# Reordering the seven products of a blocked matmul stage, with a later unit end and an earlier first store, in a fused spectral + FFN kernel

## The chip, the cores and the metric

One core of one Trainium2 chip runs the whole program. The metric is device time in microseconds from launch to end, as the median of several runs. A profile of one execution gives the span from the first to the last instruction and what each engine did in it. TensorE (PE) multiplies, VectorE (DVE) and ScalarE (ACT) do elementwise work, GpSimd (POOL) mostly issues stores, SyncE (SP) issues loads; DMAs are issued from the queues of SP, ACT and POOL. Each engine takes its instructions strictly in the order of the program.

## The reference, cut to what matters

```python
xn = layernorm(x)                                   # x: 2048 tokens x 1024
s  = irfft2(rfft2(xn) * (w_r + 1j * w_i))           # over tokens and features
h  = silu(xn @ w1)                                  # w1: 1024 x 3584
g  = silu(h @ w2)                                   # w2: 3584 x 1024
return x + s * g
```

## The kernel before

Every float32 operand is split into two float16 parts, high and low, and a product is the sum of three matmuls (high·high, high·low, low·high). The Fourier transforms are matmuls with cosine and sine tables plus butterflies on VectorE. TensorE is fed by one list of instructions that interleaves, stage after stage, the FFN with the spectral part.

**The first FFN product.** The 3584 hidden columns are 14 pairs of blocks, `q` = 0 to 13; the tokens are two halves, `g` = 0 and 1. Pairs 0 to 7 (`NPL` = 8) are computed plainly (`mm1`, line 617). Pairs 8 to 13 are computed by a seven-product scheme for a 2x2 block product: a *unit* is one (q, g), so there are 12 units, with products M1 to M7 each (`product`, line 655). A product is 12 matmuls of 512 columns; there are 84 products. This is the *seven-product stage*.

**What a unit's products need of each other.** A unit has three PSUM tiles: `a` (shown as pa), `e` (pe) and `f` (pc). M1 opens `a`; ScalarE copies it to `f` (line 667); only then may M6 add onto `a`. ScalarE copies that out (line 669) before M7 adds onto `a`; ScalarE copies that out too (line 671) before M4 adds onto `a`. M5 opens `e`, VectorE reads it (line 672), M3 adds onto it and VectorE reads it again (line 679). M2 adds onto `f`. Lines 673, 675, 677 and 680 are the Silu of the four results `h` (pool tag `h32`). PSUM tiles `a` and `e` have two buffers each, so two units can overlap.

**The unit's end.** When M3's result is in, `hidden(q, g)` forms on VectorE three differences `hr` and changes `h` in place (lines 707, 708, 710), and then splits both into high (ScalarE, line 267) and low (VectorE, line 270): the four blocks of `h` into `hoone`, the three of `hr` into `hosum`. Seven stores of 256 KB follow on the POOL queue (line 701), to `hd_one`, `hd_dif`, `hd_sum_0/1` and `hd_sum_d` in DRAM. `hoone`, `hosum` and `hr` have one buffer each.

**What sets the order.** The products stand in a hand-written order: product `name` of unit n is placed at 7·n + its number in `SLOTS`, and all are sorted by that place. After each product, `after(ev)` first runs the *turn*: `settle()` emits the evacuation of the product before, and each step that an earlier step returned, one step per turn. So a function that returns another function delays it by one turn. `tick()` runs deferred stores, and `work()` emits background steps: scaling of weight blocks (lines 267, 270, 435 to 439), maxima of the second weight matrix (`w2max_gen`: 289 on ScalarE, on loads of 256 KB from `in_B_w` into `xn`) and of the spectral weights (line 1162 on VectorE).

**The next stage.** The second FFN product is again seven products (`mm2`, lines 783 to 785, tile pb), the first of which reads only `hd_sum_d`, back from DRAM by `load_h` (line 740; the first seven issued on SP, later ones on ACT). One step of it is 21 matmuls. After five steps TensorE runs the forward transform of tokens 1024 and up (`fa_mat`, line 1016), which needs the cosine table `ca` (512 KB) loaded anew (line 1471, on SP) by `open_fd`, called in `second_half`. ScalarE takes the transform out into `fs` (line 1027). The pool `hid` (with `h32`, `hr`, `hosum`, `hoone`) is closed before that, and the pool `acc`, in which `fs` and the sums `kept` live, takes its place in SBUF.

Of the kernel before, what the change touches and what calls it, by code (L numbers as in the profile page):

```python
# [22 lines left out]
LEAD, PAUSE, EARLY = 2.5, -1, 2  # L23
NPL = 8
KB = 1024
SLOTS = (("M1", 0), ("M6", 2), ("M5", 3), ("M7", 4), ("M2", 5), ("M4", 6), ("M3", 8))
IORDER = (1, 3, 0, 2)
SUMMED, ADDED = (1, 2), (4, 5)
TURNED = (2, 3)
# [112 lines left out]
def spectral_ffn(ctx, tc, x, w_r, w_i, w1, w2, ca, kc, ci, tw, pm, out):  # L142
# [12 lines left out]
    X1 = fp.tile([128, 16 * KB], F32, name="xn")  # L155
    R3 = fp.tile([128, 7 * KB], F32, name="w1")
    hstack = ExitStack()
    H = {"p": hstack.enter_context(tc.tile_pool(name="hid", bufs=1))}
    pf = ctx.enter_context(tc.tile_pool(name="pf", bufs=4, space=PSUM))
    P = {"es": ExitStack()}  # L160
    P["t"] = P["es"].enter_context(tc.tile_pool(name="pt", bufs=2, space=PSUM))
# [25 lines left out]
    def defer(n, fn):  # L187
        deferred.append([n, fn])
# [421 lines left out]
    def mm1(c, f):  # L610
        ps = pf.tile([128, 512], F32, name=f"pa{c}_{f}", tag="ff")
        w, xt = w1t[f], xnT[c]
        terms = [(d, wh, xh) for wh, xh in ((0, 0), (0, 1), (1, 0)) for d in range(8)]
        if c + f:
            terms.sort(key=lambda k: k[0])
        for n, (d, wh, xh) in enumerate(terms):
            nc.tensor.matmul(ps, w[:, wh, d], xt[:, xh, d], start=(n == 0), stop=(n == 23))  # L617
        if c == 3:
            used1.add(f)
            done1.pop(f)()  # L620
        q, g = f // 2, c // 2

        def evac():
            if (q, g) not in h32:
                h32[q, g] = H["p"].tile([128, 4, 512], F32, name=f"h32_{q}_{g}", tag="h32", bufs=2)
            hq = h32[q, g]
            nc.scalar.activation(hq[:, 2 * (c % 2) + f % 2], ps, AF.Silu, scale=ep[:, q:q + 1])  # L627
            if c % 2 and f % 2:
                return hidden(q, g)

        return evac
# [3 lines left out]
    def product(q, g, name):  # L635
# [24 lines left out]
        act, tt = nc.scalar.activation, nc.vector.tensor_tensor  # L660

        def evac():
            if name == "M1":
                h32[q, g] = H["p"].tile([128, 4, 512], F32, name=f"h32_{q}_{g}", tag="h32", bufs=2)
            hq = h32[q, g]
            if name == "M1":
                act(f, a, AF.Copy)  # L667
            elif name == "M6":
                act(hq[:, 0], a, AF.Copy)
            elif name == "M7":  # L670
                act(hq[:, 1], a, AF.Copy)
                tt(hq[:, 1], hq[:, 1], e, op=OP.add)
                return lambda: lambda: (act(hq[:, 1], hq[:, 1], AF.Silu, scale=sc), None)[1]
            elif name == "M4":
                act(hq[:, 3], a, AF.Silu, scale=sc)
            elif name == "M2":
                act(hq[:, 2], f, AF.Silu, scale=sc)
# [6 lines left out]
    def hidden(q, g):  # L684
# [6 lines left out]
        def split(names, src):  # L691
# [5 lines left out]

            def rest():
                low(ov[1], sv, sc, ov[0])
                for k, m in enumerate(names):  # L700
                    defer(1, lambda k=k, m=m: stores[0].dma_start(  # L701
                        hd[m, g][:, :, q].rearrange("f p h s -> f p (h s)"), o[:, k].rearrange("f p h s -> f p (h s)")))

# [9 lines left out]
        summed = ("sum_0", "sum_1", "sum_d"), sums  # L713

        def second():
            a_, b_ = (one, summed) if q >= NPL else (summed, one)
            rest_a = split(*a_)

            def third():
                if q >= NPL:  # L720
                    rest_a()
                    return split(*b_)
                rest_b = split(*b_)
                rest_a()
                return rest_b

            return third

        return second

    stile, queues, fins, sstore = {}, {}, {}, {}
    part, ht = {}, {}
# [297 lines left out]
    def fd_gen(c):  # L1030
# [70 lines left out]
                yield 0  # L1101
        o, sp = {}, {}

        def high_r(j):
            sp[j] = ap.tile([128, 4, 2, 256], F16, name=f"Rs{c}_{j}", tag="Rs", bufs=2)
            nc.scalar.activation(sp[j][:, :, 0], o[j], AF.Copy, scale=2.0**-11)

        def low_r(j):
# [4 lines left out]
                queue.dma_start(vd[j][:, :, c], sp[j])  # L1113
                vcount[j] += 1

            defer(1 if c == 3 or queue is nc.scalar else 2, keep)

        for j in range(4):
            hold_x[0] = hold_x[0] or c == 1
# [346 lines left out]
    def open_fd():  # L1466
        spots = (("E", 0), ("P", 0), ("Q", 2080), ("EE", 4160), ("EO", 6240), ("DS", 8320), ("Rb", 0), ("Rd", 2048), ("Ro", 4160))
        FW[2] = FW[3] = Map({**{k: [(X1, 16 * KB + v)] for k, v in spots}, "V": [(X1, 0)], "Rs": [(X1, 16 * KB + 10400), (R2[0], 60 * KB)],
                             "L0": [(H["scr"], 0)]})
        A["ca"] = view(R2[0], 72 * KB + 256, [128, 2, 8, 128], F16)  # L1470
        nc.sync.dma_start(A["ca"], ca)

    def load_i(c):
        zt = C["p"].tile([128, 4, 2, 2, 8, 64], F16, name=f"zt{c}", tag="zt", bufs=1)
# [186 lines left out]
    with tc.manual_schedule():  # L1661
# [119 lines left out]
        plan = sorted((7 * n + o, n, name) for n in range(len(strassen)) for name, o in SLOTS)  # L1781
        w2j = None
        for n, (_, u, name) in enumerate(plan):
            q, g = strassen[u]
# [40 lines left out]
        steps = [(0, j, k) for k in range(2) for j in range(4)] + [(0, j, k) for j in range(4, 8) for k in range(2)]  # L1825
# [84 lines left out]
```

## Time and profile before

| | us |
|---|---|
| median of 3 runs | 1280.06 (1277.38 to 1281.12) |
| the profiled execution's own time | 1275.51 |
| its span | 1273.7 |
| TensorE busy | 1234.6 (97% of the span) |
| VectorE busy | 992.1 (78%) |
| ScalarE busy | 565.9 (44%) |
| POOL busy | 269.9 (21%) |

The profiled execution is a little shorter than the three timed ones; the span is 1.8 us less than its own time. TensorE matmuls are pipelined, so a product of 12 matmuls shows as 2.75 us but the next starts 2.59 us after it. In the timeline, a row is start, duration, engine, line, operation, and in brackets the idle time before it and what ended it. In the list of waits a row is the waiting instruction, what it waited for, the total, the number of times and the longest.

### The profile page before, as it was taken

The page shows a single profiled execution, that of the slowest core. Times are in us where ns is not written, and L with a number is a line of the kernel's source. Part 1 is how long each engine was busy: PE and PEld are TensorE (multiplying, and loading weights), DVE is VectorE, ACT ScalarE, POOL GpSimd, SP SyncE. Part 2 cuts the span into 40 slices and gives each one's busy share as a digit, 9 for nine tenths or more (in the row PEclk, how much of TensorE's full clock was granted, in tenths as well). Part 3 has the DMA queues.
Part 4 walks back from the last instruction along what each step waited for, and adds up shares of the span by engine and source line. Part 5 has one row for each costly group of instructions (what it writes and reads, how often), then busy time and mean ns, then how long its engine had stood idle before and what let it go on. Part 6 is the DMA issues. An engine that isn't in the chain of part 4 may idle for free. (4 is left out here: it accounts for less than half of the span.)

```text
span 1273.7 us, 18601 instructions
## 1 busy us (share of the span) xinstructions
PE 1234.6 (97%) x6827; PEld 640.0 (50%) x6827; DVE 992.1 (78%) x1646; ACT 565.9 (44%) x844; POOL 269.9 (21%) x428
## 2 busy tenths in 40 slices
PE   8999999999999998999999999999899989999998
PEld 5544444444444443444445455555455456566654
DVE  6677998889987876877487959996799338976875
ACT  4855465664447776766323223332234213412221
POOL 1221243523233231332200000202122400110111
PEclk9999999999999999999999999999899999999999
DMA  7469698867578878856946888979999998977687
GB/s 237 130 161 227 161 307 223 235 174 214 125 191 240 258 232 265 266 170 204 317 146 187 256 252 212 323 232 289 201 284 285 344 353 296 312 281 281 226 271 264
DMA packets 184187, 306.68 MB, mean 241 GB/s; under 512 B 32032, under 2 KB 92448, under 8 KB 182944
## 3 DMA queue, kind: packets, MB, share of 16 engines
q1 hardware_dynamic: 138176, 163.85, 42.9%
q0 software_dynamic: 30128, 92.82, 25.5%
q10 hardware_dynamic: 15792, 48.83, 10.9%
q8 instruction: 53, 0.87, 0.3%
q14 instruction: 38, 0.31, 0.1%
HBM read 204.25 MB, written 111.67 MB: 248 GB/s over the span
## 5 line engine op out<-in xcount | busy, mean ns | idle before, releaser
L617 PE MATMUL pa<-xn,w 128*128 128x512 f16 x1536 | 335.2, 381 | 5.8 <-DVE w L270 2.5
L783 PE MATMUL pb<-r,w 128*128 128x512 f16 (+1 forms) x798 | 299.8, 376 | 1.0 <-DMA w<-hd_one 1.0
L784 PE MATMUL pb<-r,w 128*128 128x512 f16 (+1 forms) x798 | 299.8, 376 | 0.0
L785 PE MATMUL pb<-r,w 128*128 128x512 f16 (+1 forms) x798 | 299.7, 376 | 0.0
L617 PEld LDWEIGHTS <-w 128*128 128x128 f16 x1536 | 150.1, 98 | 186.9 <-issue 3.9
L655 PEld LDWEIGHTS <-w 128*128 128x128 f16 x1008 | 98.5, 98 | 131.5 <-issue 12.5
L785 PEld LDWEIGHTS <-w 128*128 128x128 f16 x798 | 78.0, 98 | 91.2
L783 PEld LDWEIGHTS <-w 128*128 128x128 f16 x798 | 78.1, 98 | 86.9 <-DMA w<-hd_one 1.5
L784 PEld LDWEIGHTS <-w 128*128 128x128 f16 x798 | 78.0, 98 | 85.3
L655 PE MATMUL pa<-r,w 128*128 128x512 f16 x432 | 99.1, 379 | 11.0 <-ACT pc L667 7.5
L267 ACT ACTIVATE r<-r,sc 128x512 f16<-128x512 f32 x88 | 61.1, 715 | 101.4 <-DMA r<-in_B_w_dram 70.0
L270 DVE SCALAR_TENSOR_TENSOR r<-r,sc 128x512 f16<-128x512 f32 x88 | 65.1, 747 | 35.4 <-ACT r L267 35.2
L701 POOL DMA_DIRECT2D hd_one<-hoone x52 | 45.6, 876 | 199.3 <-DVE hoone L270 111.4
L701 POOL DMA_DIRECT2D hd_sum<-hosum x52 | 42.7, 932 | 158.1 <-DVE hosum L270 101.7
L270 DVE SCALAR_TENSOR_TENSOR hoone<-h,hs,hoone 128x2048 f16<-128x2048 f32 x28 | 65.7, 2345 | 8.0 <-ACT hoone L267 7.8
L267 ACT ACTIVATE hoone<-h,hs 128x2048 f16<-128x2048 f32 x28 | 55.9, 1995 | 21.7 <-DMA hd_one<-hoone 12.2
L267 ACT ACTIVATE hosum<-hr,hs 128x1536 f16<-128x1536 f32 x28 | 44.0, 1570 | 28.6 <-DVE hr L708 23.9
L627 ACT ACTIVATE h<-pa,ep 128x512 f32<-128x512 f32 x64 | 42.9, 676 | 29.5 <-PE pa L617 28.0
L270 DVE SCALAR_TENSOR_TENSOR hosum<-hr,hs,hosum 128x1536 f16<-128x1536 f32 x28 | 50.7, 1811 | 1.2 <-ACT hosum L267 1.2
L1228 PE MATMUL fx<-xn 128*128 128x256 f16 x192 | 45.2, 280 | 5.2 <-DMA xn<-vd 5.2
L1495 PE MATMUL iu<-xn 128*128 128x256 f16 x384 | 46.2, 279 | 3.2 <-DVE xn L1505 2.7
L707 DVE TENSOR_TENSOR hr<-h 128x1024 f32<-128x1024 f32 x28 | 34.2, 1220 | 17.5 <-ACT h L627 14.2
(292 smaller groups left out, 2041.4 us busy)
## 6 DMA issues: line engine op xcount, KB each, us to landing
w<-hd_dif ACTq DMA_DIRECT2D x32, 448.0 KB, 6.3
r<-in_B_w_dram SPq DMA_DIRECT2D x56, 256.0 KB, 8.6
w<-hd_sum ACTq DMA_DIRECT2D x32, 448.0 KB, 6.8
w<-hd_one ACTq DMA_DIRECT2D x32, 448.0 KB, 6.8
hd_sum<-hosum POOLq DMA_DIRECT2D x52, 256.0 KB, 5.2
hd_one<-hoone POOLq DMA_DIRECT2D x52, 256.0 KB, 4.6
hd_dif<-hoone POOLq DMA_DIRECT2D x52, 256.0 KB, 4.2
xn<-in_B_w_dram SPq DMA_DIRECT2D x40, 256.0 KB, 5.1
```

The lines of the kernel that those rows point to most:

```text
L267: nc.scalar.activation(hi, raw, AF.Copy, scale=scale)
L270: nc.vector.scalar_tensor_tensor(lo, raw, scale, hi, op0=OP.mult, op1=OP.subtract)
L617: nc.tensor.matmul(ps, w[:, wh, d], xt[:, xh, d], start=(n == 0), stop=(n == 23))
L627: nc.scalar.activation(hq[:, 2 * (c % 2) + f % 2], ps, AF.Silu, scale=ep[:, q:q + 1])
L655: nc.tensor.matmul(ps, lhs(d, wh), rhs(d, xh), start=(name in ("M1", "M5") and d + n == 0), stop=(d + n == 5), skip_group_check=True)
L701: defer(1, lambda k=k, m=m: stores[0].dma_start(hd[m, g][:, :, q].rearrange("f p h s -> f p (h s)"), o[:, k].rearrange("f p h s -> f p (h ...
L707: tt(sums[:, 0:2], hq[:, 0::2], hq[:, 1::2], op=OP.subtract)
L783: nc.tensor.matmul(ps, hh[:, 0], w[:, 0], start=first, stop=False)
L784: nc.tensor.matmul(ps, hh[:, 0], w[:, 1], start=False, stop=False)
L785: nc.tensor.matmul(ps, hh[:, 1], w[:, 0], start=False, stop=last)
L1228: nc.tensor.matmul(o, k[:, c, kh, 1], v[:, c, vh], start=(n == 0), stop=False)
L1495: nc.tensor.matmul(ps[:, q], lhs, rhs, start=(n == 0 and r == 0), stop=(n == 2 and r == 1))
```

## The change

`SLOTS` gets other numbers. Taken in turn, a unit n in mid-stage went M1(n), M3(n-1), M6(n), M5(n), M7(n), M2(n), M4(n); now it goes M1(n), M4(n-1), M3(n-1), M6(n), M5(n), M7(n), M2(n). `FINAL`, used for the last unit, holds the same numbers. `h` is allocated at M6 and not at M1. `hidden` returns its splitting step one turn later for the pairs from 8 on; for the last unit it splits `hosum` ahead of `hoone`; within `hosum` the store to `hd_sum_d` comes first, for all units. The cosine table is asked for in `second_half` once `ready2` is 11 and not 13, with one pause fewer afterwards. The pool `hid` is split: `h32` stays in it, the rest goes to a pool `ho` behind it; and `fs` gets a pool of its own, `scr`, ahead of `acc`. `kept_r` makes sure that the store of a spectral tile is issued before its buffer is written again.

```diff
-SLOTS = (("M1", 0), ("M6", 2), ("M5", 3), ("M7", 4), ("M2", 5), ("M4", 6), ("M3", 8))
+SLOTS = (("M1", 0), ("M6", 3), ("M5", 4), ("M7", 5), ("M2", 6), ("M4", 8), ("M3", 9))
+FINAL = (("M1", 0), ("M6", 3), ("M5", 4), ("M7", 5), ("M2", 6), ("M4", 8), ("M3", 9))
...
-    H = {"p": hstack.enter_context(tc.tile_pool(name="hid", bufs=1))}
+    H = {"h": hstack.enter_context(tc.tile_pool(name="hid", bufs=1)), "p": hstack.enter_context(tc.tile_pool(name="ho", bufs=1))}
...
-            if name == "M1":
-                h32[q, g] = H["p"].tile([128, 4, 512], F32, name=f"h32_{q}_{g}", tag="h32", bufs=2)
-            hq = h32[q, g]
+            if name == "M6":
+                h32[q, g] = H["h"].tile([128, 4, 512], F32, name=f"h32_{q}_{g}", tag="h32", bufs=2)
+            hq = h32.get((q, g))
...
-                for k, m in enumerate(names):
+                for k, m in sorted(enumerate(names), key=lambda t: t[1] != "sum_d"):
                     defer(1, lambda k=k, m=m: stores[0].dma_start(
...
-            a_, b_ = (one, summed) if q >= NPL else (summed, one)
+            a_, b_ = (one, summed) if q >= NPL and (q, g) != (NP - 1, 1) else (summed, one)
             rest_a = split(*a_)
             def third():
-                if q >= NPL:
+                if a_ is one:
                     rest_a()
                     return split(*b_)
...
-        return second
+        return (lambda: second) if q >= NPL else second
...
+        kept_r = {}
+
         def high_r(j):
+            if j - 2 in kept_r:
+                kept_r.pop(j - 2)()
...
-        A["ca"] = view(R2[0], 72 * KB + 256, [128, 2, 8, 128], F16)
-        nc.sync.dma_start(A["ca"], ca)
...
     def second_half():
-        while not p2[0] or ready2[0] < 13:
+        while not p2[0] or ready2[0] < 11:
+            yield PAUSE
+        A["ca"] = view(R2[0], 72 * KB + 256, [128, 2, 8, 128], F16)
+        nc.sync.dma_start(A["ca"], ca)
+        yield PAUSE
+        while ready2[0] < 13:
             yield PAUSE
         open_fd()
-        for _ in range(3):
+        for _ in range(2):
             yield PAUSE
...
-        for _ in range(6):
+        for _ in range(7):
             settle()
             tick()
         hstack.close()
         reopen("pu")
         H["es"] = ExitStack()
+        scr_pool = H["es"].enter_context(tc.tile_pool(name="scr", bufs=1))
+        H["scr"] = scr_pool.tile([128, 2080], F32, name="fs")
         acc_pool = H["es"].enter_context(tc.tile_pool(name="acc", bufs=1))
-        H["scr"] = acc_pool.tile([128, 2080], F32, name="fs")
```

How the instructions then stand, at three places. A name is tile_q_g_serial, or tile_buffer_serial; line numbers after the change are up to a few higher for the same statement (671 is 672, 289 is 290).

ScalarE before, from the copy of M7 of unit (11, 1) to the copy of M6 of unit (12, 0):

```order
L671 ACTIVATE h_11_1_4457<-pa_1_4420 128x512
L267 ACTIVATE hoone_11_0_4538<-h_11_0_4302,hs 128x16x128
L677 ACTIVATE h_11_1_4457<-pc_1_4422,ep 128x512
L267 ACTIVATE hosum_11_0_4556<-hr_0_4515,hs 128x12x128
L289 ACTIVATE both,ma<-r_2498 128x512 x2
L675 ACTIVATE h_11_1_4457<-pa_1_4420,ep 128x512
L673 ACTIVATE h_11_1_4457<-h_11_1_4457,ep 128x512
L289 ACTIVATE both,ma<-r_2498 128x512 x2
L667 ACTIVATE pc_0_4570<-pa_0_4568 128x512
L289 ACTIVATE both,w2m<-xn 128x512 x2
L669 ACTIVATE h_12_0_4606<-pa_0_4568 128x512
```

Here `hosum`, two Silus and two pairs of 289 stand between the split of `hoone` and M1's copy (667). ScalarE at the same place after:

```order
L672 ACTIVATE h_11_1_4498<-pa_1_4397 128x512
L678 ACTIVATE h_11_1_4498<-pc_1_4399,ep 128x512
L268 ACTIVATE hoone_11_0_4559<-h_11_0_4342,hs 128x16x128
L290 ACTIVATE both,ma<-r_2501 128x512 x2
L668 ACTIVATE pc_0_4545<-pa_0_4543 128x512
L674 ACTIVATE h_11_1_4498<-h_11_1_4498,ep 128x512
L268 ACTIVATE hosum_11_0_4582<-hr_0_4518,hs 128x12x128
L290 ACTIVATE both,ma<-r_2501 128x512 x2
L676 ACTIVATE h_11_1_4498<-pa_1_4397,ep 128x512
L290 ACTIVATE both,w2m<-xn 128x512 x2
L670 ACTIVATE h_12_0_4646<-pa_0_4543 128x512
```

M1's copy (now 668) has moved ahead of the Silu of M7, of `hosum`, of a pair of 290 and of the Silu of M4; these now stand between it and the copy of M6 (670).

POOL before, the last unit's stores, with the last one of the unit ahead of it:

```order
L701 DMA hd_sum_d_82<-hosum_13_0_5120 512x1x256
L701 DMA hd_one_1_93<-hoone_13_1_5151 512x1x256
L701 DMA hd_dif_1_85<-hoone_13_1_5151 512x1x256
L701 DMA hd_dif_1_87<-hoone_13_1_5151 512x1x256
L701 DMA hd_one_1_91<-hoone_13_1_5151 512x1x256
L701 DMA hd_sum_1_95<-hosum_13_1_5154 512x1x256
L701 DMA hd_sum_1_89<-hosum_13_1_5154 512x1x256
L701 DMA hd_sum_d_83<-hosum_13_1_5154 512x1x256
```

Here `hd_sum_d` is the last of all. POOL at the same place after:

```order
L702 DMA hd_sum_0_91<-hosum_13_0_5138 512x1x256
L702 DMA hd_sum_d_86<-hosum_13_1_5154 512x1x256
L702 DMA hd_sum_1_98<-hosum_13_1_5154 512x1x256
L702 DMA hd_sum_1_92<-hosum_13_1_5154 512x1x256
L702 DMA hd_one_1_96<-hoone_13_1_5156 512x1x256
L702 DMA hd_dif_1_88<-hoone_13_1_5156 512x1x256
L702 DMA hd_dif_1_90<-hoone_13_1_5156 512x1x256
L702 DMA hd_one_1_94<-hoone_13_1_5156 512x1x256
```

The store of `hd_sum_d` has moved from seventh to first of the last unit's seven. SP before, around the cosine table:

```order
L740 DMA w_67<-hd_sum_d_82 128x1792 x4
L555 DMA r_2498<-wt_4_154 128x512
L555 DMA r_2498<-wt_5_155 128x512
L1471 DMA r_2498<-in_ca_dram 128x2048
L555 DMA r_2498<-wt_6_156 128x512
```

and after:

```order
L741 DMA w_67<-hd_sum_d_85 128x1792 x4
L556 DMA r_2501<-wt_4_157 128x512
L556 DMA r_2501<-wt_5_158 128x512
L1655 DMA r_2501<-in_ca_dram 128x2048
L556 DMA r_2501<-wt_6_159 128x512
```

The load of the table stands behind the same four loads of `hd_sum_d` and the same two of `wt` as before; on SP nothing has moved here. On TensorE nothing has moved outside the seven-product stage.

More of the change, by code (lines that the diff above doesn't have):

```diff
@@ L662, in evac @@
         def evac():
-            if name == "M1":
-                h32[q, g] = H["p"].tile([128, 4, 512], F32, name=f"h32_{q}_{g}", tag="h32", bufs=2)
-            hq = h32[q, g]
+            if name == "M6":
+                h32[q, g] = H["h"].tile([128, 4, 512], F32, name=f"h32_{q}_{g}", tag="h32", bufs=2)
+            hq = h32.get((q, g))
             if name == "M1":
@@ L1114, in keep @@
                 vcount[j] += 1
-            defer(1 if c == 3 or queue is nc.scalar else 2, keep)
+            kept_r[j] = keep
+            defer(1 if c == 3 or queue is nc.scalar else 2, lambda: kept_r.pop(j, int)())
         for j in range(4):
@@ L1780, in spectral_ffn @@
         strassen = [(q, g) for q in range(NPL, NP) for g in range(2)]
-        plan = sorted((7 * n + o, n, name) for n in range(len(strassen)) for name, o in SLOTS)
+        plan = sorted((7 * n + o, n, name) for n in range(len(strassen)) for name, o in (SLOTS if n + 1 < len(strassen) else FINAL))
         w2j = None
```

## The prediction

> **What bounds the kernel now.** I read the page's first part to see which engine is the bound.
>
> ```profile
> span 1273.7 us, 18601 instructions
> ...
> PE 1234.6 (97%) x6827; PEld 640.0 (50%) x6827; DVE 992.1 (78%) x1646; ACT 565.9 (44%) x844; POOL 269.9 (21%) x428
> ```
>
> TensorE is idle for 1273.7 − 1234.6 = 39.1 us, and the change takes away no matmul. So everything that it can win lies in those 39 us, and it wins it only where TensorE stops waiting. The second view is TensorE's list of waits, which says for what it stops.
>
> ```profile
> PE pa L655 <- ACT pc L667: 7.5, 5, 2.7
> PE fx L1228 <- DMA xn<-vd: 5.2, 2, 5.0
> PE iu L1495 <- DVE xn L1505: 2.7, 1, 2.7
> ...
> PE fa L1016 <- DMA r<-in_ca_dram: 2.3, 1, 2.3
> PE pa L655 <- ACT h L669: 2.0, 2, 1.2
> ...
> PE pa L655 <- ACT h L671: 1.5, 1, 1.5
> ```
>
> Four of these six rows are in reach of the diff. Line 655 is the seven-product stage: five stops of M6 for M1's copy (667), two of M7 for M6's copy (669), one of M4 for M7's copy (671), 11.0 us in all. Line 1016 is the transform that waits for the cosine table. The third view is TensorE's timeline over the stage: its ends, and the stops of which I speak below.
>
> ```profile
> 374.29 2.75 PE L655 MATMUL pa<-xn,w 128*128 128x512 f16 x12
> ...
> 377.77 2.76 PE L655 MATMUL pa<-r,w 128*128 128x512 f16 x12 [0.73 <-ACT pc L667]
> ...
> 403.38 2.75 PE L655 MATMUL pa<-r,w 128*128 128x512 f16 x12 [1.25 <-ACT h L669]
> ...
> 485.38 2.75 PE L655 MATMUL pa<-r,w 128*128 128x512 f16 x12 [1.54 <-ACT h L671]
> ...
> 534.34 2.75 PE L655 MATMUL pa<-r,w 128*128 128x512 f16 x12 [2.71 <-ACT pc L667]
> ...
> 601.68 2.75 PE L655 MATMUL pe<-xn,w 128*128 128x512 f16 x12
> 604.27 0.38 PE L783 MATMUL pb<-r,w 128*128 128x512 f16 x1
> ```
>
> The stage takes 604.27 − 374.29 = 229.98 us. A product that nothing disturbs takes 604.27 − 601.68 = 2.59, and 84 of them 217.56. So 12.4 us are lost here, of which the waits name 11.0; the other 1.4 over eight stops are 0.18 each, in which the pipeline of matmuls fills again.
>
> Why the copy is late is seen on ScalarE ahead of the longest stop, at 534.34.
>
> ```profile
> 525.85 2.00 ACT L267 ACTIVATE hoone<-h,hs 128x2048 f16<-128x2048 f32 x1 [3.54 <-DVE h L710]
> 527.76 0.67 ACT L677 ACTIVATE h<-pc,ep 128x512 f32<-128x512 f32 x1
> 528.33 1.56 ACT L267 ACTIVATE hosum<-hr,hs 128x1536 f16<-128x1536 f32 x1
> 529.79 0.62 ACT L289 ACTIVATE both<-r 128x512 f16<-128x512 f32 x1
> ...
> 531.16 0.67 ACT L675 ACTIVATE h<-pa,ep 128x512 f32<-128x512 f32 x1
> 531.73 0.71 ACT L673 ACTIVATE h<-h,ep 128x512 f32<-128x512 f32 x1
> 532.35 0.62 ACT L289 ACTIVATE both<-r 128x512 f16<-128x512 f32 x1
> ...
> 533.72 0.58 ACT L667 ACTIVATE pc<-pa 128x512 f32<-128x512 f32 x1
> ```
>
> ScalarE first stands 3.54 us for `hidden`'s last difference (710), and then works without a gap until the copy. TensorE asked for that copy at 534.34 − 2.71 = 531.63.
>
> **The change, part by part.**
>
> *The order of the seven products.* M6 keeps its place in the row, and M1 moves one product ahead of where it was: M4 now stands behind M1 and not ahead of it. So M1's copy has two products, 5.2 us, and had one. M7's copy likewise has two (M2 and M1 of the next unit) before M4, and had one. M6's copy still has one, M5, before M7. I walk the heaviest boundary, above, through the new order of ScalarE, with starts differenced from its rows. The split of `hoone` starts no sooner than 525.85, since the products that `hidden` follows have not moved, and takes 527.76 − 525.85 = 1.91; a pair of 289 takes 531.16 − 529.79 = 1.37; then the copy, 0.58, is done at 527.76 + 1.37 + 0.58 = 529.7. M6's turn is at 531.63: 1.9 us to spare, and 0.5 where a second pair stands there. So the 667 stops go, apart from the 0.73 at 377.77, which is the first unit, with no unit ahead of it to move behind: 7.5 − 0.7 = 6.8. The 671 stop at 485.38 goes too, 1.5: the added product is 2.59 and the stop 1.54. With five stops go five refills, 5 x 0.18 = 0.9. Together **−9.2**.
>
> What is late next is the copy of M6, because the work that stood ahead of 667 now stands behind it. Behind 529.7 come a Silu (673) 0.62, the split of `hosum` 1.46, a pair 1.37, a Silu (675) 0.57, a pair 1.37 and the copy 0.58: 535.7. M6 itself, 2.75 long, ends at 534.4, and M7's turn is at 531.63 + 2 x 2.59 = 536.8. That leaves 1.1 us, and −0.3 where another pair falls in between. The stop at 403.38 stays: 289 there waited for a load, as its row says, and 669 is behind it in both orders.
>
> ```profile
> 402.13 0.63 ACT L289 ACTIVATE both<-xn 128x512 f16<-128x512 f32 x1 [1.25 <-DMA xn<-in_B_w_dram]
> ```
>
> For the new M7 waits the trace has no row. Below: none, if each boundary is like the one walked. Above: two like 403.38 and one extra pair, 2 x 1.25 + 1.37 = 3.9. I take **+0.7**, two stops of 0.3 each with some refill, as only boundaries with a pair more than the walked one are short.
>
> *The unit's end one turn later.* The splits then no longer stand in ScalarE's row at the moment when 710 is still running, so the 3.54 us of standing go into useful work; the walk has that in it. The stores follow a product, 2.59, later, and `hoone` and `hosum`, with one buffer each, are taken again 18 us later (seven products), so they hide. `h` allocated at M6 moves no instruction: zero.
>
> *The last unit's end and the cosine table.* Here is the end of the stage, on SP, POOL, ScalarE and TensorE, with the time from the table's issue to its landing.
>
> ```profile
> 604.25 10.02 SPq L740 DMA_DIRECT2D w<-hd_sum_d  x4
> ...
> 615.61 0.43 SPq L1471 DMA_DIRECT2D r<-in_ca_dram  x1
> ```
>
> ```profile
> 615.31 0.71 POOL L701 DMA_DIRECT2D hd_one<-hoone  x1 [6.81 <-DVE hoone L270]
> ...
> 619.08 1.36 POOL L701 DMA_DIRECT2D hd_sum_d<-hosum  x1
> ```
>
> ```profile
> 613.01 1.58 ACT L267 ACTIVATE hosum<-hr,hs 128x1536 f16<-128x1536 f32 x1 [0.38 <-DMA hd_sum_d<-hosum]
> ...
> 629.87 0.72 ACT L267 ACTIVATE r<-r,sc 128x512 f16<-128x512 f32 x1 [12.84 <-DMA hd_sum_d<-hosum]
> ```
>
> ```profile
> 629.44 0.22 PE L1016 MATMUL fa<-r,xn 128*128 128x128 f16 x1 [2.35 <-DMA r<-in_ca_dram]
> ```
>
> ```profile
> DMA to landing us min/median/max: 13.7/13.7/13.7
> ```
>
> ```profile
> 620.00:625.00 5.00, 5.00 (x25) 2.26 (x24) 0.00 (x0) 0.00 (x0) 0.44 (x1) 1.00 1.02 380
> ```
>
> SP cannot go past the loads of `hd_sum_d` until that block is stored, 604.25 to about 613, and the table's load stands behind them. The order shows it at the same place after: asking when `ready2` is 11 moves nothing on SP, so the edit by itself is worth zero. What changes is what lies beside it. The table is issued at 615.61 and lands 13.7 later, at 629.3, because the DMA engines are full (share 1.02 in the last row) with the last unit's seven stores, issued from 615.31, among others. After, `hd_sum_d` of the unit ahead is stored as first of its three, and not as last, so SP is free at least as soon. The last unit's split of `hosum`, now first, can still not start before its buffer's stores land, near 613.0; 1.58 on ScalarE and about as much on VectorE put the first store 1 to 2 us later than 615.31, and the four `hoone` stores some 3 us behind the first. So the table's load has the queues to itself for its first microseconds. Bounds for its landing time: 13.7 again, and the median of loads of the same 512 KB elsewhere:
>
> ```profile
> w<-in_B_w_dram SPq DMA_DIRECT2D x17, 512.0 KB, 6.1
> ```
>
> TensorE comes at 629.44 − 2.35 = 627.1, 11.5 us after the issue. The middle of 6.1 and 13.7 is 9.9, which is in time. So the stop goes with its refill: **−2.5**; at 13.7 it stays.
>
> A rule of the Trainium skill bears on this, "DMA: Bandwidth & Descriptors", section "Queues, rings and completion order": each DMA engine takes turns, packet by packet, between the queue rows that have work for it. By it the table on SP's row shared with POOL's row almost from its issue before, and has less to share with afterwards, so the stop would go (−11.0 in all); by the one row there is, 13.7, it would stay (−8.5). The share of 1.02 agrees that the engines were full; no row tells whose packets went first.
>
> The store of `hd_sum_d` as the last unit's first ends ScalarE's 12.84 us of standing early. That costs TensorE nothing now, since ScalarE's next work for it (1027) follows the stopped 1016, and it gains nothing by itself. Splitting the pools lets `fs` be cleared without waiting for those stores: VectorE only, hidden behind the five steps of `mm2` that TensorE does meanwhile, zero; and if that cover went, it is no more than the 2.35 already counted. The seventh turn puts an `mm2` step ahead of the pool's closing only in program order, not on TensorE: zero. `kept_r` issues a store at the latest when its buffer is rewritten; behind the stage it moves nothing on SP's or POOL's queue: zero.
>
> Sum: −9.2 − 2.5 + 0.7 = **−11.0 us**. The profiled execution took 1275.51, so it would take 1264.5; it lies 4.55 below the median of 1280.06, and from the median the forecast is **1269**.
>
> **The rivals.**
>
> *The table stays late.* It lands 13.7 us after its issue again, or the loads that share SP's queue hold it. Then the −2.5 falls away: −8.5, 1271.6. For it: the DMA engines stay full, since all the bytes still have to move. Against it: the stores start later.
>
> *Given back later.* All that follows starts 11 us sooner, but loads do not get faster. The next long stop is for a load:
>
> ```profile
> 917.37 0.37 PE L1228 MATMUL fx<-xn 128*128 128x256 f16 x1 [5.03 <-DMA xn<-vd]
> ```
>
> ```profile
> 918.00:920.00 2.00, 2.00 (x16) 1.73 (x15) 1.35 (x2) 0.86 (x2) 0.17 (x1) 0.50 1.08 320
> 950.00:1000.00 50.00, 50.00 (x266) 25.07 (x265) 39.75 (x66) 15.15 (x28) 21.98 (x45) 1.00 0.99 305
> ```
>
> The engines are full at 950 to 1000 (share 0.99), and after a stop of 5.03 the granted clock is 0.50. If that stretch is set by its bytes, the stop grows by what is gained ahead of it: all 11 us come back, and one more spell at half clock, some 2 us, may come with it: 1278 to 1282, middle 1280. For it: the stop is there and the engines are full. Against it: TensorE is busy 97%, so the loads mostly keep up, and what feeds this stop is issued when earlier work on the same engines is done, which moves forward with it.
>
> *Slower: M7 waits in every unit.* The moved work stands ahead of 669 at all 11 boundaries, and each pair of 289 may itself wait for its load.
>
> ```profile
> ACT h L671 <- PE pa L655: 21.5, 9, 4.0
> ACT h L669 <- PE pa L655: 16.3, 9, 4.0
> ACT both L289 <- DMA xn<-in_B_w_dram: 10.3, 6, 4.8
> ```
>
> The walk left 1.1 us. For the result to be slower than before by 0.3% (3.84 us, about what a measurement of this kernel can tell from no change) the new waits must come to 11.0 + 0.7 + 3.8 = 15.5, 1.4 per boundary, so ScalarE must be 2.5 us later than in the walk at each: 1284 or more. For it: six waits of 289 for a load, up to 4.8 us. Against it: at nine of the 12 units ScalarE stood at 669 waiting for TensorE, 16.3 / 9 = 1.8 us each, so it is ahead there at most boundaries.
>
> **How the numbers follow.** The forecast, 1269, gets 0.66; the table still late, 1271.6, 0.13; given back, 1280, 0.14; slower, 1284 or more, 0.04; 0.03 is for a gain larger than I can see. The forecast's own range: M7 waits from 0 to 3.9 in place of 0.7 give 1268.3 to 1272; the scatter of the three runs, 1277.4 to 1281.1, adds 2 or 3 us on each side. From 1263 to 1277 holds the first two cases and the smaller part of "given back". Faster by over 0.3% is below 1276.2: the first two, the last, and a small part of the third: 0.84. Within 0.3%: 0.11. Slower: 0.05.
>
> **What would show it.** In the trace after, the 667 row of TensorE's waits should hold one stop of 0.7; the 671 row should be gone; 669 should hold 2 to 5 stops and under 4 us; from the stage's first product to the first `mm2` matmul should be 221 to 222 us. The load of the table should be issued about 11 us after that point and land within 11.5 us, with no stop at 1016. The `vd` stop at 1228 should be about 5 us still. The prediction is wrong if the 669 row rises above 4 us or the stops in 850 to 1050 grow by what the stage gained.

## The result, and the profile after

The changed kernel takes 1269.15 us (median of 9 runs, 1266.86 to 1271.73); the kernel before, over nine runs, 1278.55. The ratio is 0.9931, with a 95% interval of 0.9916 to 0.9947: 8.8 us faster, between 6.8 and 10.7. Measured a second time, the same kernel gave 1269.98 and a ratio of 0.9935 (0.9913 to 0.9957).

TensorE is again read first, by the page's first part:

```profile
span 1265.8 us, 18607 instructions
...
PE 1232.4 (97%) x6827; PEld 639.3 (51%) x6827; DVE 991.6 (78%) x1646; ACT 567.0 (45%) x844; POOL 272.5 (22%) x428
```

The span fell by 1273.7 − 1265.8 = 7.9 us. TensorE's list of waits from the stage's start to past the transform has only two rows left (line numbers are one higher than before):

```profile
PE pa L656 <- ACT pc L668: 2.6, 2, 1.9
PE pa L656 <- ACT h L670: 2.2, 4, 0.8
```

The row for M7's copy (671 before) and the row for the cosine table are gone. In TensorE's timeline, the stage's ends, the stops that matter and the transform:

```profile
375.96 2.75 PE L656 MATMUL pa<-xn,w 128*128 128x512 f16 x12
379.44 2.76 PE L656 MATMUL pa<-r,w 128*128 128x512 f16 x12 [0.73 <-ACT pc L668]
...
492.65 2.75 PE L656 MATMUL pa<-r,w 128*128 128x512 f16 x12 [1.87 <-ACT pc L668]
...
599.27 0.38 PE L784 MATMUL pb<-r,w 128*128 128x512 f16 x1
...
621.93 0.22 PE L1017 MATMUL fa<-r,xn 128*128 128x128 f16 x1
```

The 7.9 us divide into four stretches. The stage takes 599.27 − 375.96 = 223.31, and took 229.98: −6.7. From its end to the transform it is 621.93 − 599.27 = 22.66, and was 629.44 − 604.27 = 25.17: −2.5. Ahead of the stage it is 375.96 − 374.29 = +1.7, where the edit moves nothing on TensorE, and behind the transform 643.87 against 644.26: −0.4. The last two are within the scatter of profiles: over the fourteen of this study the stage begins between 373.56 and 376.45, and a second profile of the changed kernel began its stage at 375.40, took 222.31 for it, 22.66 to the transform and 645.83 behind it.

The table's load (SP), the last unit's first store (POOL) and the load's time to landing:

```profile
610.44 0.38 SPq L1655 DMA_DIRECT2D r<-in_ca_dram  x1
```

```profile
613.34 0.71 POOL L702 DMA_DIRECT2D hd_sum_d<-hosum  x1 [8.65 <-DVE hosum L271]
```

```profile
DMA to landing us min/median/max: 10.2/10.2/10.2
```

Counted from the stage's end, the load is issued at 11.2 us (before 11.3), the stores start at 14.1 (before 11.0), and the table lands at 21.4, ahead of TensorE at 22.7.

### The profile page after: what moved, and what is told of

Read it like the earlier page. It is cut to its first block, busy times and chain, and to the rows that moved or that the text cites. A ratio compares the mean times of both kernels' runs of the same rounds, so it can differ in the third digit from the quotient of the medians.

```text
span 1265.8 us, 18607 instructions
## 1 busy us (share of the span) xinstructions
PE 1232.4 (97%) x6827; PEld 639.3 (51%) x6827; DVE 991.6 (78%) x1646; ACT 567.0 (45%) x844; POOL 272.5 (22%) x428
## 5 line engine op out<-in xcount | busy, mean ns | idle before, releaser
L268 ACT ACTIVATE hoone<-h,hs 128x2048 f16<-128x2048 f32 x28 | 55.8, 1994 | 14.1 <-DMA hd_one<-hoone 8.0
L702 POOL DMA_DIRECT2D hd_sum_d<-hosum x26 | 23.6, 907 | 165.3 <-DVE hosum L271 107.9
L708 DVE TENSOR_TENSOR hr<-h 128x1024 f32<-128x1024 f32 x28 | 34.2, 1220 | 14.3 <-ACT h L628 13.1
```

The lines of the kernel that those rows point to most:

```text
L268: nc.scalar.activation(hi, raw, AF.Copy, scale=scale)
L702: defer(1, lambda k=k, m=m: stores[0].dma_start(hd[m, g][:, :, q].rearrange("f p h s -> f p (h s)"), o[:, k].rearrange("f p h s -> f p (h ...
```

## Experiments

The first question was which part of the edit is worth what. Each of its main parts was done alone on the kernel before, or undone alone in the changed kernel; the table's earlier request and `kept_r` were not run by themselves. The stage runs from its first product to the first `mm2` matmul in each profile, in us, and "to transform" from there to the first matmul of line 1016. These two columns come from one execution each; the ratio comes from several runs.

| kernel | stage | to transform | ratio of times to before |
|---|---|---|---|
| before | 229.98 | 25.17 | 1 |
| changed | 223.31 | 22.66 | 0.9931 (0.9916 to 0.9947) |
| changed, second profile | 222.31 | 22.66 | 0.9935 (0.9913 to 0.9957) |
| order alone | 229.43 | 24.21 | 0.9974 (0.9954 to 0.9995) |
| changed, old order | 230.37 | 22.66 | 0.9977 (0.9956 to 0.9998) |
| changed, old turn of the unit's end | 229.14 | 22.67 | 0.9966 (0.9949 to 0.9984) |
| last unit's sums first, alone | 230.52 | 22.66 | 1.0009 (0.9987 to 1.0031) |
| changed, last unit's sums as before | 224.99 | 25.76 | 0.9976 (0.9961 to 0.9991) |
| changed, old pools | 224.30 | 22.66 | 0.9961 (0.9938 to 0.9985) |
| two products in all hand-overs | 232.72 | 27.79 | 1.0039 (1.0018 to 1.0061) |
| changed, without maxima in the stage | 222.15 | 22.66 | 0.9887 (0.9857 to 0.9918) |
| changed, maxima one step later | 224.12 | 22.66 | 0.9906 (0.9882 to 0.9930) |

**The order alone.**

```diff
-SLOTS = (("M1", 0), ("M6", 2), ("M5", 3), ("M7", 4), ("M2", 5), ("M4", 6), ("M3", 8))
+SLOTS = (("M1", 0), ("M6", 3), ("M5", 4), ("M7", 5), ("M2", 6), ("M4", 8), ("M3", 9))
```

> The kernel before with the new order of the seven products alone (and h allocated at M6). Theory: the stage loses most of its stops for 667 and 671 by the order alone, so from its first product to the first mm2 matmul it takes 222 to 225 us (before 229.98, after the change 223.31), the stop for the cosine table stays at 2 to 3 us, and the time is 5 to 7 us below before. Rival: the order alone does little, because without the later unit end the split of hoone still stands on ScalarE waiting for line 710 ahead of M1's copy; then the stage stays at 227 to 230 us and the time within 3 us of before.

The rival held for the stage: it is 229.43, 0.6 us shorter than before. The time is 2.9 us below before by the medians, at the edge of the rival's 3. The order takes 3.1 us off the stops for M1's copy (7.5 before), but those for M6's copy grow by 2.7 (2.0 before; TensorE's waits):

```profile
PE pa L655 <- ACT h L669: 4.7, 3, 1.9
PE pa L655 <- ACT pc L667: 4.4, 5, 1.9
```

ScalarE at the boundary from unit (11, 1) to (12, 0):

```profile
527.90 2.00 ACT L267 ACTIVATE hoone<-h,hs 128x2048 f16<-128x2048 f32 x1 [3.16 <-DVE h L710]
529.81 0.67 ACT L677 ACTIVATE h<-pc,ep 128x512 f32<-128x512 f32 x1
530.38 1.56 ACT L267 ACTIVATE hosum<-hr,hs 128x1536 f16<-128x1536 f32 x1
...
533.22 0.58 ACT L667 ACTIVATE pc<-pa 128x512 f32<-128x512 f32 x1
```

ScalarE stands 3.16 us for line 710, and both splits are still ahead of M1's copy. The extra product covers some of it, but not this. In the whole stage ScalarE stands 13.7 us for line 710, and stood 7.6 before.

**The later unit end alone**, that is, the changed kernel with the old `SLOTS` in place (`FINAL` likewise).

```diff
-SLOTS = (("M1", 0), ("M6", 3), ("M5", 4), ("M7", 5), ("M2", 6), ("M4", 8), ("M3", 9))
+SLOTS = (("M1", 0), ("M6", 2), ("M5", 3), ("M7", 4), ("M2", 5), ("M4", 6), ("M3", 8))
```

> The changed kernel with the old order of the seven products; later unit end, last unit, pools as changed. Theory (order and later end are worth something only together): the split of hosum and two pairs of line 290 still stand ahead of M1's copy with one product to cover them, so the stage stays at 226 to 230 us, the transform's stop stays away, and the time is 3 to 6 us above the changed kernel's. Rival (the later end alone does it, since ScalarE no longer stands waiting for line 711): the stage is at 222 to 225 us.

The theory held. The stops for M1's copy are as large as in the kernel before (7.5):

```profile
PE pa L656 <- ACT pc L668: 7.4, 5, 2.6
PE pa L656 <- ACT h L670: 2.7, 2, 1.8
```

ScalarE's waits in the stage no longer hold a row for `hidden`'s last difference (711 here), but the split of `hosum` (here 492.36) still precedes the copy (495.19), which has one product to cover it:

```profile
492.36 1.56 ACT L268 ACTIVATE hosum<-hr,hs 128x1536 f16<-128x1536 f32 x1
...
495.19 0.58 ACT L668 ACTIVATE pc<-pa 128x512 f32<-128x512 f32 x1
```

**The later unit end undone.**

```diff
-        return (lambda: second) if q >= NPL else second
+        return second
```

> The changed kernel with the unit's end at its old turn (the split steps not one turn later). Theory: the split of hoone stands on ScalarE waiting for line 711 ahead of M1's copy again, at some of the boundaries, so 668 stops of 1 to 3 us in total come back and the stage takes 224 to 226 us; the table's stop stays away; the time is 0 to 3 us above the changed kernel's. Rival: the added product covers that as well, and the stage stays at 223.3 or below, with the stops left being those of line 290 for its loads.

The theory had the direction and too small a size: the stage is back at 229.14, 5.8 us above the changed kernel's. ScalarE stands 15.5 us for line 711 (4.0 in the changed kernel), and stops of all three kinds are there again (TensorE's waits):

```profile
PE pa L656 <- ACT pc L668: 4.9, 5, 1.9
PE pa L656 <- ACT h L670: 4.0, 3, 1.6
PE pa L656 <- ACT h L672: 1.2, 1, 1.2
```

So in the stage the order and the later end gain 0.6 and −0.4 us each by itself, less than the 1.0 by which two profiles of the changed kernel differ, and 6.7 together. The order alone leaves ScalarE standing for line 710; the later end alone leaves `hosum` ahead of a copy that one product covers. Of these kernels, only the changed one has `hosum` behind M1's copy at the boundaries near 492 and 527.

**The last unit's sums first, alone.**

```diff
-                for k, m in enumerate(names):
+                for k, m in sorted(enumerate(names), key=lambda t: t[1] != "sum_d"):
...
-            a_, b_ = (one, summed) if q >= NPL else (summed, one)
+            a_, b_ = (one, summed) if q >= NPL and (q, g) != (NP - 1, 1) else (summed, one)
```

> The kernel before with the last unit's sums split and stored first and hd_sum_d stored first of the sums; order of the products, unit's end and pools as before. Theory (the table lands in time because the last unit's stores start later): the sums must wait for their buffer, so the stores start 1 to 3 us later than 11.0 us after the stage's end, the table lands in 9 to 12 us and its stop of 2.35 us falls to 0 to 1.2; the stage stays at 230, the time is 1 to 2.5 us below before. Rival (the table's earlier request or the split pools did it): the stop stays at 2 to 2.5 us and the time is that of before.

The theory held for the table: it lands 10.0 us after its issue, and that stop is gone. It failed for the time, which is that of before. TensorE's next matmul for the transform stops instead, because VectorE clears `fs`, and ScalarE then copies into it, only when the last store of `hd_one` has landed (VectorE's and TensorE's timelines):

```profile
631.31 0.10 DVE L1026 MEMSET fs<- 128x8 f32 x2 [9.51 <-DMA hd_one<-hoone]
```

```profile
632.48 0.22 PE L1016 MATMUL fa<-r,xn 128*128 128x128 f16 x1 [2.83 <-ACT fs L1028]
```

**The last unit's sums as before, in the changed kernel.**

```diff
-                for k, m in sorted(enumerate(names), key=lambda t: t[1] != "sum_d"):
+                for k, m in enumerate(names):
...
-            a_, b_ = (one, summed) if q >= NPL and (q, g) != (NP - 1, 1) else (summed, one)
+            a_, b_ = (one, summed) if q >= NPL else (summed, one)
```

> The changed kernel with the last unit's four blocks of h split and stored first and hd_sum_d last, as before; the later unit end, the table's request and the pools stay changed. Theory (the stores' start decides): the stores start sooner than 14.1 us after the stage's end, at 11 to 12.5, the table's landing goes back to 12 to 14 us and a stop of 1 to 2.5 us at the transform returns; the time is 1 to 2.5 us above the changed kernel's. Rival (the later unit end alone delays the stores enough, or the split pools did it): no stop, same time as the changed kernel.

The theory held, with a larger stop than it gave. From the stage's end (599.40) the stores start at 11.9 us and the table is asked for at 12.5; it takes 13.1 to land, and TensorE stops for it:

```profile
611.29 0.71 POOL L702 DMA_DIRECT2D hd_one<-hoone  x1 [6.48 <-DVE hoone L271]
```

```profile
DMA to landing us min/median/max: 13.1/13.1/13.1
```

```profile
PE fa L1017 <- DMA r<-in_ca_dram: 2.9, 1, 2.9
```

The later unit end is in this kernel, so it isn't what holds the stores back; the order of the sums is. The time rose by 4 to 6 us, against the 1 to 2.5 expected: the stretch up to the transform (25.76 against 22.66) explains 3.1, and the stage of this one profile is 1.7 to 2.7 longer than in the two of the changed kernel, for which no cause was looked for.

**The pools as before, in the changed kernel.**

```diff
-    H = {"h": ...tile_pool(name="hid", bufs=1)), "p": ...tile_pool(name="ho", bufs=1))}
+    H = {"p": ...tile_pool(name="hid", bufs=1))}
+    H["h"] = H["p"]
...
-        H["scr"] = scr_pool.tile([128, 2080], F32, name="fs")
+        H["scr"] = acc_pool.tile([128, 2080], F32, name="fs")
```

> The changed kernel with the pools as before: one pool for h, hr and the splits, and fs in the pool acc. Theory (from the run with the last unit's sums first alone, where TensorE stopped 2.83 us at the transform for fs, whose clearing on VectorE waited for the last store of hd_one): the table lands in time, and a stop of 2 to 3.5 us at the transform for the copy into fs takes its place; the time is 2 to 4 us above the changed kernel's. Rival (the prediction's zero for this part): no stop there, the time is that of the changed kernel.

The theory held. `fs` shares its pool with tiles that take the place of those still being stored, and waits for them; TensorE stops for it at the transform (VectorE's timeline; TensorE's waits):

```profile
627.48 0.10 DVE L1028 MEMSET fs<- 128x8 f32 x2 [9.22 <-DMA hd_one<-hoone]
```

```profile
PE fa L1018 <- ACT fs L1030: 3.5, 1, 3.5
```

In the changed kernel the clearing waits for no store. The stop is 3.5 us; the time, against the changed kernel's second measurement on the same chip, is 0.9961 to 0.9935, some 3 us, with intervals that overlap.

**Two products in all three hand-overs.** A try at a better order.

```diff
-SLOTS = (("M1", 0), ("M6", 3), ("M5", 4), ("M7", 5), ("M2", 6), ("M4", 8), ("M3", 9))
+SLOTS = (("M1", 0), ("M6", 3), ("M5", 5), ("M7", 6), ("M2", 8), ("M4", 9), ("M3", 11))
```

> The changed kernel with an order of the products in which all three hand-overs (M1 to M6, M6 to M7, M7 to M4) have two products between: M1(n), M2(n-1), M4(n-1), M6(n), M3(n-1), M5(n), M7(n). Theory (what is left of the stage's stops is one product too little of cover at M7, and loads that line 290 waits for): the 670 stops go but for the first unit, M1's copy stands right behind M7's on ScalarE so the 668 stop near 492 goes, the stage takes 218.5 to 221.5 us and the time is 2 to 5 us below the changed kernel's. Rival (the later M3 pushes the unit's end and its stores into the next unit's hand-overs, or makes TensorE wait for h or for pe): the stage stays at 222 to 226 us and the time is that of the changed kernel or above.

The rival held, by more than it gave: the stage, 232.72, is above its 226, and the kernel is slower than before. Of the longer stretch to the transform, 4.5 us are a sixth step of `mm2` that TensorE does there, in place of five. The stops moved to M7 (TensorE's waits, then ScalarE ahead of the longest, at 462.99):

```profile
PE pa L656 <- ACT h L670: 11.0, 5, 4.0
```

```profile
446.05 0.58 ACT L668 ACTIVATE pc<-pa 128x512 f32<-128x512 f32 x1 [0.88 <-PE pa L656]
449.69 0.63 ACT L290 ACTIVATE both<-r 128x512 f16<-128x512 f32 x1 [3.06 <-DMA r<-in_B_w_dram]
...
453.13 0.63 ACT L290 ACTIVATE both<-xn 128x512 f16<-128x512 f32 x1 [1.97 <-DMA xn<-in_B_w_dram]
...
462.36 0.58 ACT L670 ACTIVATE h<-pa 128x512 f32<-128x512 f32 x1
```

Between the two copies ScalarE now has four pairs of 290, both splits and three Silus, and stood 5.0 us for loads: together more than the two products cover.

**The changed kernel again**, with no edit.

> The changed kernel itself once more, for the scatter of its stops. Theory: the stops at the same three or four places of the stage (near 385, 404 and 492 us) come again, within 1 us in total, since the loads that line 290 waits for come in the same order; stage 222.5 to 225 us, no stop at the transform. Rival: the stop near 492 is chance and goes; stage 221 to 222 us.

The theory held: stops at 384.74, 403.88 and 491.52, the last of 1.90. The small ones near 478 and 534 did not come again, and the stage, 222.31, is 0.2 us under the range.

**Without the maxima.** Two kernels, the changed one and the one with two products in all hand-overs, put constants in place of the results of line 290 by writes on VectorE where the maxima stood.

```diff
-            magnitude(t_.rearrange("p a b -> p (a b)"), w2m[:, 2 * n:2 * n + 2])
+            nc.vector.memset(w2m[:, 2 * n:2 * n + 2], 1.0)
...
-                magnitude(r[i].rearrange("p a b -> p (a b)"), ma[:, 2 * i:2 * i + 2])
+                nc.vector.memset(ma[:, 2 * i:2 * i + 2], 1.0)
```

> The changed kernel without the absolute maxima on ScalarE (the pairs of line 290) of the second weight matrix and of the first one's last blocks in the stage; constants stand in their place, the loads stay. Theory (what is left of the stage's stops is ScalarE standing in those pairs for their loads): the 668 stop near 492 and the 670 stops go, apart from the first unit's 0.7 at 668 and at most 0.5 at 670; the stage takes 218 to 219.5 us. Rival (the splits and Silus behind M1's copy are themselves too long for M7): 670 stops stay, and the stage takes 220.5 to 222 us.

> The order with two products in all three hand-overs, also without those maxima (constants in their place, loads kept). Theory (that order lost because the pairs of line 290 come to stand between M1's and M6's copies and wait there for their loads): its 670 stops of 4.0, 3.0 and 2.1 us go, the stage takes 218 to 220 us and not 232.7. Rival (the splits of hoone and hosum and the Silus alone make M6's copy late): 670 stops of 1 us and more stay, the stage is above 222.

Neither tells what it was meant to. The stages are 228.07 and 234.02, single times 1271.78 and 1284.54, and ScalarE came to wait for those very writes, which stand in VectorE's row behind its own waits (ScalarE's waits in the first):

```profile
ACT h L670 <- DVE w2m L477: 5.1, 1, 5.1
```

So the constants were set once at the program's start, and nothing was written in the stage:

```diff
     w2m = small("w2m", 2 * NFT)
+    nc.vector.memset(w2m, 1.0)
...
-            magnitude(t_.rearrange("p a b -> p (a b)"), w2m[:, 2 * n:2 * n + 2])
+            pass
...
-                magnitude(r[i].rearrange("p a b -> p (a b)"), ma[:, 2 * i:2 * i + 2])
+                pass
```

> The changed kernel without the maxima of line 290 in the stage, as in after_no_maxima, but with nothing written in their place there (the constants are set once, at the program's start), since in that run ScalarE and TensorE came to wait for the constants' writes on VectorE. The loads stay. Theory (what is left of the stage's stops is ScalarE standing in those pairs for their loads): the 668 stop near 492 goes, the 670 stops go but for the first unit's, the stage takes 218 to 220 us and the time is 2 to 5 us below the changed kernel's. Rival (the splits and Silus alone, or buffers of h that come free late, make the copies late): stops of more than 1 us stay behind the first unit, the stage takes 221 us or more.

It came out between the two. The stop near 492 is gone, so that one is the maxima's. Three stops for M6's copy stayed behind other causes (TensorE's waits, then ScalarE's):

```profile
PE pa L657 <- ACT h L671: 3.2, 3, 1.7
```

```profile
ACT h L671 <- DVE hoone L272: 10.6, 4, 5.6
...
ACT hoone L269 <- DMA hd_one<-hoone: 3.4, 2, 3.1
```

M6's copy (671 here) writes the buffer of `h` that VectorE's split of two units ago must have read, and that split is late. The stage, 222.15, is no shorter than the changed kernel's. The ratio, 0.9887, is lower than its 0.9931, with intervals that just touch; where that time was won, the stage doesn't show.

**The maxima one step later**, a try at that stop.

```diff
+            if not early:
+                yield 0
             size(n, d_)
```

> The changed kernel with one more empty step between the load of a block of the second weight matrix and its maximum, so that line 290 comes a turn later than now against its load. Theory: ScalarE waits less for these loads, the 668 stop near 492 shrinks below 1 us, the stage takes 220 to 222 us and the time is 0 to 3 us below the changed kernel's. Rival: the maxima only move to other places in ScalarE's row, where another copy is late; stage and time as the changed kernel's, or up to 4 us above.

Not settled. The profile shows the rival (TensorE's waits: the stop near 492 went, and one of 2.7 us came near 527), while the time, 1266.77 and 0.9906, is a little below the changed kernel's, with intervals that overlap:

```profile
PE pa L658 <- ACT pc L670: 3.4, 2, 2.7
```

## Why the prediction was right, and where it was not

**The time.** 1269 was forecast and 1269.15 measured, but the gain was forecast as 11.0 and measured as 8.8. The three runs of before that the forecast started from lie 1.5 us above the median of nine; this made up for most of the rest. That the two times agree so closely is luck; the gain was a fifth smaller than forecast.

**The stops for 667** were to fall by 6.8 to the first unit's 0.7; they fell by 4.9, to 2.6. The first unit's stop came exactly (0.73). The step that failed is the walk of one boundary, the one with the longest stop, as if it bounded the others. It wasn't the one with the most work: before, ScalarE had two pairs of 289 between the split of `hosum` and M1's copy there (from 529.79 and 532.35), and three at the boundary that comes near 492 after the change (from 489.15, 490.65 and 493.21). For a boundary with a second pair ahead of the copy the walk left 0.5 us. Near 492 two pairs are ahead of it after the change (in ScalarE's row), and they wait for loads:

```profile
487.83 0.63 ACT L290 ACTIVATE both<-r 128x512 f16<-128x512 f32 x1 [1.75 <-DMA r<-in_B_w_dram]
...
490.24 0.63 ACT L290 ACTIVATE both<-xn 128x512 f16<-128x512 f32 x1 [0.93 <-DMA xn<-in_B_w_dram]
...
491.40 0.63 ACT L290 ACTIVATE both<-xn 128x512 f16<-128x512 f32 x1 [0.44 <-DMA xn<-in_B_w_dram]
...
492.03 0.58 ACT L668 ACTIVATE pc<-pa 128x512 f32<-128x512 f32 x1
```

That is 3.1 us of standing, and the stop is 1.87. The kernel without maxima has no stop there, so these pairs are the cause; that it is their loads, and not their own work, is argued from 3.1 being more than 1.87, and was not tested by itself. The list of ScalarE's waits before had a row for the loads into `xn`, 10.3 us with 4.8 as its longest; the prediction counted it for M7 and not for M6. The 1.75 is for a load into `r`, for which ScalarE didn't wait in the stage before.

**The new stops of M7** were put at +0.7 for the row of 669; it went from 2.0 to 2.2, in four stops (forecast: 2 to 5, under 4 us). At the walked boundary the walk left 1.1 us for M6's copy and 1.9 for M1's; the copies stood at

```profile
527.87 0.58 ACT L668 ACTIVATE pc<-pa 128x512 f32<-128x512 f32 x1
...
533.89 0.58 ACT L670 ACTIVATE h<-pa 128x512 f32<-128x512 f32 x1
```

against M6 at 528.91 and M7's turn at 534.25: 0.5 to spare and 0.3 late. The walk was 1.4 us too kind in both: the split of `hoone` began 5.0 us ahead of M6's turn and not 5.8, and a load cost 0.6. In the second profile there is no stop at this place, and the row of 670 is 1.4, in two stops.

**The stop for 671 and the refills** went as forecast: 1.5, and the stage's loss is 223.31 − 217.56 = 5.8, of which 4.8 is named. The stage should have come to 221 to 222 and came to 223.3 and 222.3.

**The later unit end.** It was priced within the walk, and the text called the order the cause of the 9.2. The runs showed that neither does anything alone. The walk was right about the pair because it went through the new row of ScalarE, which has both in it. It was not right that the later end turns all of the standing for 710 into work: there is less of it, 4.0 us in place of 7.6, and still 1.87 at the walked boundary:

```profile
523.90 2.00 ACT L268 ACTIVATE hoone<-h,hs 128x2048 f16<-128x2048 f32 x1 [1.87 <-DVE h L711]
```

**The table.** −2.5 came as −2.5, and not by the earlier request (11.3 to 11.2 us, nothing) but by the order of the last unit's sums: the two runs above show that, one each way. That they act through stores that start later, as forecast, is argued. The start at 14.1 us was 3 later and not 1 to 2. Where the stores start with the request or up to 0.6 us before it, the table lands in 12.8 to 13.7 us (three profiles), and where they start 2.7 to 3.4 us behind it, in 8.7 to 10.2 (nine). By the Trainium skill, "DMA: Bandwidth & Descriptors", section "Queues, rings and completion order", each DMA engine takes the queue rows that have work for it in turn, packet by packet. These twelve profiles agree with what was worked out from it. The start of the stores isn't all, though. With two products in all hand-overs they start 3.2 us ahead of the request, and the table lands in 7.4 us (7.1 in that order without the maxima); SP's and POOL's timelines:

```profile
620.62 1.27 SPq L741 DMA_DIRECT2D w<-hd_sum_d  x3
...
629.47 1.00 SPq L1655 DMA_DIRECT2D r<-in_ca_dram  x1
```

```profile
626.28 0.71 POOL L702 DMA_DIRECT2D hd_sum_d<-hosum  x1 [8.10 <-DVE hosum L271]
```

There the loads of `hd_sum_d`, ahead of the table on SP's own queue, were issued 7.6 us or more before it; in the kernel before and in the changed one the last of those on SP came less than 2 us before it. Whether that is the reason was not tested.

**The pools** were put at zero, with the words that a lost cover would cost no more than the 2.35 already counted. That step was wrong. In the kernel before, VectorE's timeline shows that `fs` was cleared just when the table came, so the table's stop hid this one:

```profile
629.55 0.10 DVE L1026 MEMSET fs<- 128x8 f32 x2 [10.15 <-DMA hd_sum_d<-hosum]
```

With the table in time and the old pools, 2.83 to 3.5 us stand there. Not all of that was hidden before: with the sums first, the stores that hold `fs` end later too, so it is cleared 631.31 − 604.15 = 27.2 us after the stage's end, and before at 629.55 − 604.27 = 25.3. By these two rows about 2.83 − 1.9 = 0.9 us was hidden behind the table's stop (an estimate), and the later stores added the rest. Two waits that end at nearly the same time show as one. The new pools alone, on the kernel before, were not run.

**Given back later** did not happen as a whole. The `vd` transform (line 1228, 5.2 before) now shows

```profile
PE fx L1234 <- DVE r L271: 2.9, 1, 2.9
...
PE fx L1234 <- DMA xn<-vd: 1.2, 1, 1.2
```

4.1 in all, and the stretch behind the transform is 0.4 us shorter. In the second profile of the same kernel the stop is 7.3, 2.1 above before, and the stretch 1.6 us longer. In the other profiles of this study the stop is 3.6 to 10.3 us, whatever the edit; part of the scatter between runs may come from there, which was not tested.

**The slower mechanism**, M7 waiting in every unit, is real: an order that looked safer by its count of products ran into it, 11.0 us of stops. At the walked boundary the changed kernel was already 0.3 us into it in one of its two profiles.

## What to carry to other kernels

When a copy is late, walk the whole row of the engine that makes it, at every boundary and with the waits for loads in it, and not only count the products that cover it: a reordering and a delay that gain almost nothing in the stage each can gain together. When a stop goes, ask which other wait ended at the same moment behind it; here the table and the clearing of `fs` ended about 0.2 us apart, and getting the table in time was worth nothing until `fs` had its own pool. Background work that waits for its own load does not belong between a product and the copy that the next product needs.

## What the runs showed of the hardware

The changed kernel's stretches around the table's load (the last two columns are the share of the DMA engines and GB/s) show the engines as full as they were in the kernel before from 615 to 625 (1.01 and 1.02):

```profile
610.00:615.00 5.00, 5.00 (x25) 2.25 (x23) 3.70 (x2) 5.00 (x6) 1.66 (x3) 1.00 1.02 392
615.00:620.00 5.00, 5.00 (x25) 2.26 (x24) 3.16 (x7) 0.54 (x1) 3.46 (x5) 1.00 1.00 359
```

Yet a 512 KB load's landing time went with 3 us in the start of other transfers: 8.7 to 10.2 us in nine profiles where it was issued about 3 us ahead of seven stores of 256 KB, 12.8 to 13.7 us in three where it was issued with them or just behind the first. In two more it landed in 7.1 and 7.4 us although it was issued 3.2 us behind the first store, so what is queued ahead of a load may matter as much as what comes behind it. I had expected the full engines to matter more than the order of issue.
